# Reordering the first steps of a DeltaNet + hardswish kernel: second norms behind the first group's last score, the inverse's result through SP's queue, query loads between evictions

## The chip, the cores and the metric

The kernel runs on one core of a Trainium2 chip. The metric is device time in microseconds (us). Kernels are compared only within the same rounds.

## The reference

A delta-rule recurrence over 768 tokens, for 4 batches and 8 heads of dimension 48, and then a hardswish MLP over the 3072 resulting tokens (384 to 2048 to 384).

```python
k_n = k / (np.linalg.norm(k, axis=-1, keepdims=True) + 1e-06)
for t in range(S):
    kt, vt, bt = (k_n[:, :, t], v[:, :, t], beta[:, :, t, None])
    y[:, :, t] = np.einsum('bhd,bhde->bhe', q[:, :, t], state)
    v_old = np.einsum('bhde,bhd->bhe', state, kt)
    state = state + bt[:, :, :, None] * np.einsum('bhd,bhe->bhde', kt, vt - v_old)
# ... y, transposed to (tokens, 384), is x
h = x @ w_in
g = h * np.clip(h + 3.0, 0.0, 6.0) / 6.0
out = g @ w_out
```

## The kernel before

The tokens are cut into 24 steps of 32, and the steps into groups of `GS = 4`. Each step has a preparation (`prep`: POOL scales keys, PE transposes keys and queries, ACT copies the transposes out of PE's output memory into `KQ`, which I call evicting, PE makes scores, DVE masks them into `LB`; `kb` are the scaled keys and `mb` the mask times beta, both made by POOL). Each group has its key norms (`norms`) and one triangular inverse on DVE (`inverse`), which collects the group's four `LB` in DRAM, loads them as one matrix `A`, and sends the result back through DRAM (`x_dram`) into the same four `LB`. Then `chain(t)` runs the recurrence; its first matrix product is called `pz`, and `R` is the DVE subtraction that starts every step but the first. The MLP's weights arrive in a format of eight bytes and are converted on the fly by `convert()`: five DVE operations (e, m, m, e and w_in or w_out, after what they write) and one ACT operation (on e) for each of 16 pieces. Steps are counted from 0. `take(x, n)` emits n parts of a generator and `drain(x)` the rest; the order of emission is each engine's order. `need(n)` emits conversions until n are done.

The end of the inverse, and the opening of the program:

```python
def inverse(g, dma):
    ...
    dma.dma_start(out=x_dram[g]..., in_=A...)
    for i in range(GS):
        dma.dma_start(out=LBv[:, :, 0, :], in_=x_dram[g][i]...)
    yield
# ...
for t in range(GS):
    load_k(t)
    load_q(t, nc.scalar)            # all query loads ahead of everything on ACT
for t in range(GS):
    load_k(GS + t)
for i in range(3):
    load_w(i, early)
drain(norms(0, 0, 1))
first = [prep(t, nc.scalar) for t in range(GS)]
take(first[0], 3)
drain(norms(0, 1, GS - 1))
take(first[1])
take(first[0])
inv1 = norms(1, 0, GS)
for t in range(1, GS):
    if t + 1 < GS:
        take(first[t + 1])
    take(first[t], 2)
    if t == 2:
        drain(inv1)                 # second group's norms, ahead of LB(2)
    if t == 3:
        take(conv, 3)
    take(first[t])                  # score and LB(t)
# ...
inv = inverse(0, nc.scalar)         # A, x and its reloads on ACT's queue
take(inv)
need(2)
# ... preps of steps 4 and 5, LB(4)
take(inv, 10)
# ... LB(5)
take(inv, 12)
take(conv)
drain(inv)
take(prep_of(GS + 2), 2)            # transposes and evictions behind the inverse
# ... conversions, preps of steps 6 and 7, chain(0), chain(1)
for n in range(GS):
    load_k(2 * GS + n)              # the third group's keys
need(4)
```

Of the kernel before, what the change touches and what calls it, by code (L numbers as in the profile page):

```python
# [8 lines left out]
FP32 = mybir.dt.float32  # L9
U32 = mybir.dt.uint32  # L10
ACTF = mybir.ActivationFunctionType
# [6 lines left out]
def kernel(  # L18
# [20 lines left out]
    nc = tc.nc  # L39
# [5 lines left out]
    N = S // C  # L45
    NP = H // 2
    GS = 4
# [8 lines left out]
    const = ctx.enter_context(tc.tile_pool(name="const", bufs=1))  # L56
# [8 lines left out]
    def rows(b):  # L65
        return slice(C * b, C * b + C)
# [8 lines left out]
    def tokens(ap, b, t):  # L75
        return ap[b, :, t * C : (t + 1) * C, :].rearrange("h t d -> t h d")
# [10 lines left out]
    def load_q(t, eng=nc.sync):  # L87
        if t < N:
            for b in range(B):
                eng.dma_start(out=qbufs[t % NQB][rows(b), :, 0:D], in_=tokens(q, b, t))  # L90
# [19 lines left out]
    for j, value in enumerate((1.0, -1.0)):  # L110
        m = mask2[:, j, :]
        for b in range(B):
            nc.gpsimd.memset(mask2[rows(b), j, :], value)
            nc.gpsimd.affine_select(
                out=mask2[rows(b), j, :], in_=mask2[rows(b), j, :], pattern=[[1, C]],
                compare_op=ALU.is_gt, fill=0.0, base=0, channel_multiplier=-1,
            )
    half = const.tile([128, 1], FP32, name="half")
    nc.vector.memset(half[:], 0.5)

    beta_tok = persist.tile([P, N, C], FP32, name="beta_tok")
    nc.vector.transpose(out=beta_tok[:].rearrange("p n h -> p (n h)"), in_=beta_hm[:])
# [122 lines left out]
    l_dram, x_dram = {}, {}  # L245
# [57 lines left out]
        KQs[t], LBs[t] = KQ, LB  # L303
        yield

    def inverse(g, dma):

        A = work.tile([128, C, C], FP32, name="A", bufs=1)
        dma.dma_start(
            out=A[:].rearrange("p c i -> p (c i)"),  # L310
            in_=l_dram[g][:].rearrange("t h (b c) i -> (t h b) (c i)", b=B),
        )
        yield
        for j in range(1, C - 1):
            n = C - 1 - j
            pr = work.tile([128, C * C // 4 - C // 2], FP32, name="pr", bufs=1)
            pv = pr[:, 0 : j * n].rearrange("p (c i) -> p c i", c=j)
            nc.vector.tensor_tensor(  # L318
                out=pv, in0=A[:, j, j + 1 :].unsqueeze(1).to_broadcast([128, j, n]),
                in1=A[:, 0:j, j].unsqueeze(2).to_broadcast([128, j, n]), op=ALU.mult,  # L320
            )
            nc.vector.tensor_tensor(  # L322
                out=A[:, 0:j, j + 1 :], in0=A[:, 0:j, j + 1 :], in1=pv, op=ALU.subtract
            )
            yield
        nc.vector.memset(A[:].rearrange("p c i -> p (c i)")[:, 0 : C * C : C + 1], -1.0)
        dma.dma_start(
            out=x_dram[g][:].rearrange("t h (b c) i -> (t h b) (c i)", b=B),
            in_=A[:].rearrange("p c i -> p (c i)"),
        )  # L330
        for i in range(GS):
            LBv = LBs[g * GS + i][:].rearrange("p e a j w -> p (e a) j w")
            dma.dma_start(out=LBv[:, :, 0, :], in_=x_dram[g][i].rearrange("h p c -> p h c"))
        yield


# [115 lines left out]
    def up(blk):  # L452

        xT = xTs[blk]
        for f in range(NFC):
            ph = psM.tile([128, TB], FP32, name="ph", tag="pm")
            for s in range(NKT):
                nc.tensor.matmul(  # L458
                    ph[:], lhsT=w_in[:, s, f * 128 : (f + 1) * 128], rhs=xT[:, s, :],
                    start=(s == 0), stop=(s == NKT - 1),  # L460
                )
            t1 = mlp[0].tile([128, TB], FP32, name="t1", bufs=3)
            nc.scalar.activation(  # L463
                out=t1[:], in_=ph[:], func=ACTF.Relu, bias=half[:, 0:1], scale=1.0 / 6.0
            )
            g = mlp[0].tile([128, TB], FP32, name="g", bufs=NFC + 2)
            nc.vector.scalar_tensor_tensor(  # L467
                out=g[:], in0=t1[:], scalar=1.0, in1=ph[:], op0=ALU.min, op1=ALU.mult
            )
            gs[blk, f] = g  # L470
            yield
# [40 lines left out]
    def need(n):  # L512
        while done[0] < n:
            take(conv)


    def chained(*gens):
        for gen in gens:
            yield from gen

    def take(gen, n=1):
        for _ in range(n):
            next(gen, None)

    def drain(gen):
        for _ in gen:
            pass

    conv = convert()
# [3 lines left out]
    def prep_of(t):  # L533
        if t not in preps:
            preps[t] = prep(t, nc.sync) if t < N else iter(())
        return preps[t]

    with tc.manual_schedule():
        with tc.tile_pool(name="early", bufs=3) as early:
            for t in range(GS):  # L540
                load_k(t)
                load_q(t, nc.scalar)
            for t in range(GS):
                load_k(GS + t)
            for i in range(3):
                load_w(i, early)
            drain(norms(0, 0, 1))
            first = [prep(t, nc.scalar) for t in range(GS)]
            take(first[0], 3)
            drain(norms(0, 1, GS - 1))  # L550
            take(first[1])
            take(first[0])
            inv1 = norms(1, 0, GS)
            for t in range(1, GS):
                if t + 1 < GS:
                    take(first[t + 1])
                take(first[t], 2)
                if t == 2:
                    drain(inv1)
                if t == 3:  # L560
                    take(conv, 3)
                take(first[t])
            load_v(0)
            load_v(1)
            load_w(3)
            inv = inverse(0, nc.scalar)
            take(inv)
            need(2)
            for t in range(2):
                take(prep_of(GS + t), 3)  # L570
            take(prep_of(GS))
            take(inv, 10)
            take(prep_of(GS + 1))
            load_w(4)
            take(inv, 12)
            take(conv)
            drain(inv)
            take(prep_of(GS + 2), 2)
            take(conv)
            take(prep_of(GS + 3), 2)  # L580
            take(conv)
            for t in range(2, GS):
                take(prep_of(GS + t), 2)
                take(conv)
            for t in range(CB):
                load_v(t + 2)
                for _ in chain(t):
                    take(conv)
            for n in range(GS):
                load_k(2 * GS + n)  # L590
            need(4)
        mlp.append(ctx.enter_context(tc.tile_pool(name="mlp", bufs=2)))
        units = mlp_units()
        fill = chained(norms(2, 0, GS), inverse(1, nc.sync))
        for t in range(CB, N):
            g, i = divmod(t, GS)
            load_v(t + 2)
            if i == 1 and (g + 2) * GS < N:
                for n in range(GS):
                    load_k((g + 2) * GS + n)  # L600
            if i == 2 and t > CB:
                drain(fill)
                fill = chained(
                    norms(g + 2, 0, GS) if (g + 2) * GS < N else iter(()),
                    inverse(g + 1, nc.sync) if (g + 1) * GS < N else iter(()),
                )

            now = [prep_of(t + GS + i), prep_of(t + GS + i + 1)] if i < 2 else None
            j = (i + 1) % GS
            later = prep_of(t + 1 + GS + j) if j < 2 else iter(())  # L610
            early = t < GS
            plan = {
                0: lambda: (take(ch), now and take(now[1])),
                2: lambda: now and take(now[1]),
                3: lambda: (take(ch), now and take(now[0])),
                5: lambda: now and take(now[1]),
                7: lambda: (take(ch), now and take(now[1])),
                9: lambda: take(ch),
                11: lambda: take(ch),
                12: lambda: take(later),  # L620
                13: lambda: take(later),
                15: lambda: take(later),
            }
            ch = chain(t)
            for u in range(NU):
                if u in plan:
                    plan[u]()
                if early and u % 2:
                    continue
                if early:  # L630
                    need(min(NWI, ((t - CB) * NU + u) // 4 + 2))
                else:
                    take(conv, 2)
                if early:
                    take(fill, 3)
                take(units)
                if not early:
                    take(fill, 1 + (u % 2 == 0))
            drain(ch)
        drain(units)  # L640
# [30 lines left out]
```

## Time and profile before

| what | us |
|---|---|
| median of the first three runs (779.21 to 779.71) | 779.55 |
| span of the profiled run | 778.0 |
| inverse of the first group: first operation, store of x issued | 48.47, 74.23 |
| first pz of the chain | 84.99 |
| R of step 5, the start of the saturated part | 205.42 |

How to read it: after about 205 us PE is full, so whatever happens earlier is worth only what it moves that moment. The way there is a relay: norms, keys, scores, LB, inverse, chain. A moment of this relay (the start of the inverse, the first pz) is a better ruler than any engine's busy share.

### The profile page before, as it was taken

The numbers are of one execution on the slowest core, as the hardware profiler recorded it, in microseconds if no ns is written. First come the engines' busy times: TensorE is split into PE (matmuls) and PEld (weight loads), VectorE is DVE, ScalarE is ACT, GpSimd is POOL, SyncE is SP. The second block draws the span as 40 slices with busy tenths as digits, with TensorE's granted clock in tenths as the row PEclk, the third lists the DMA queues.
The fourth block names the chain that finished last, engine by engine and source line by source line (L and its number), as shares of the span: only waits on it lengthen the run. The fifth ranks groups of instructions, "written<-read, shape, count | busy, mean of one in ns | idle before, by whom it ended". The sixth has DMA issues, their size and how long they took to land.

```text
span 778.0 us, 24919 instructions
## 1 busy us (share of the span) xinstructions
PE 681.3 (88%) x11208; PEld 501.7 (64%) x11208; DVE 359.1 (46%) x868; ACT 178.0 (23%) x353; POOL 94.8 (12%) x139
## 2 busy tenths in 40 slices
PE   1440686668799999999999999999999999999997
PEld 1330565546576776876876867867868768677674
DVE  6498459968527831247711367511464213021020
ACT  1210321222321231321322311313213113122120
POOL 4750031003004002012011040020000000000000
PEclk9755577789999999999999999999999999999999
DMA  6653740366321131330132501311203010000000
GB/s 122 174 126 89 135 119 7 112 162 187 63 43 52 23 77 35 74 63 18 43 67 44 110 9 27 66 26 30 47 12 81 8 27 6 13 13 0 21 1 20
DMA packets 140139, 45.77 MB, mean 59 GB/s; under 512 B 130272, under 2 KB 133344, under 8 KB 140032
## 3 DMA queue, kind: packets, MB, share of 16 engines
q1 hardware_dynamic: 127008, 41.18, 23.4%
q10 hardware_dynamic: 13024, 2.98, 1.8%
q8 instruction: 88, 1.44, 0.8%
q14 instruction: 19, 0.16, 0.1%
HBM read 33.13 MB, written 11.01 MB: 57 GB/s over the span
## 4 chain that ended last, share of the span: by engine, by line
PE 74%; DVE 14%; DMA 4%; issue 3%; SPq 2%; POOL 2%; ACT 1%; ACTq 0%; POOLq 0%; DVEq 0%
PE po L479 31%; PE ph L458 29%; DVE A L322 3%; DVE pr L318 3%; PE pz L370 2%; PE py L370 2%; PE su L427 2%; PE sc L286 2%; PE ks L360 2%; PE pt L273 2%; DMA kf<-in_k_dram 2%; PE py L360 2%; DVE m L179 1%; DVE e L183 1%; DVE e L168 1%
## 5 line engine op out<-in xcount | busy, mean ns | idle before, releaser
L458 PE MATMUL ph<-xT,w_in 128*128 128x256 f32 x1152 | 277.1, 393 | 15.2 <-DVE w_in L188 9.0
L479 PE MATMUL po<-w_out,g 128*128 128x384 f32 x768 | 265.1, 494 | 4.0 <-DVE w_out L188 4.0
L458 PEld LDWEIGHTS ph<-xT,w_in 128*128 128x128 f32 x1152 | 218.4, 195 | 49.8 <-DVE w_in L188 9.4
L479 PEld LDWEIGHTS po<-w_out,g 128*128 128x128 f32 x768 | 141.3, 191 | 90.3 <-issue 5.2
L467 DVE SCALAR_TENSOR_TENSOR g<-t,ph 128x256 f32<-128x256 f32 x192 | 80.5, 420 | 189.8 <-ACT t L463 189.5
L463 ACT ACTIVATE t<-ph,half 128x256 f32<-128x256 f32 x192 | 90.7, 473 | 189.5 <-PE ph L458 176.2
L322 DVE TENSOR_TENSOR A<-A,pr 128x30 f32<-128x30 f32 (+9 forms) x180 | 68.0, 378 | 6.2
L318 DVE TENSOR_TENSOR pr<-A 128x30 f32<-128x30 f32 (+9 forms) x180 | 66.9, 372 | 4.3
L286 PE MATMUL sc<-KQ 64*32 64x64 f32 x1536 | 22.9, 249 | 43.2 <-ACT KQ L276 42.5
L435 DVE TENSOR_TENSOR state<-state,su 128x384 f32<-128x384 f32 x46 | 23.2, 546 | 71.0 <-PE su L427 71.0
L286 PEld LDWEIGHTS sc<-KQ 64*32 64x32 f32 x1536 | 18.5, 117 | 47.2 <-ACT KQ L276 45.3
L276 ACT ACTIVATE KQ<-pt 128x512 f32<-128x512 f32 x48 | 27.8, 596 | 84.5 <-PE pt L273 64.4
L258 POOL TENSOR_TENSOR mb<-beta_tok,mask 128x256 f32<-128x256 f32 x48 | 32.9, 706 | 82.7 <-DVE LB L292 82.7
L292 DVE TENSOR_TENSOR LB<-sc,mb 128x512 f32<-128x512 f32 x24 | 16.4, 685 | 57.3 <-PE sc L286 57.3
L251 POOL TENSOR_TENSOR kb<-kf,inv 128x384 f32<-128x384 f32 x24 | 21.6, 900 | 163.5 <-PE pt L273 134.1
L209 POOL TENSOR_TENSOR sq<-kf 128x384 f32<-128x384 f32 x21 | 17.4, 827 | 177.8 <-DMA kf<-in_k_dram 101.5
L485 ACT ACTIVATE o<-po 128x384 f32<-128x384 f32 x24 | 11.8, 491 | 111.5 <-PE po L479 111.5
L273 PE MATMUL pt<-ident,kb 128*128 128x128 f32 x96 | 18.3, 320 | 18.7 <-POOL kb L251 17.6
L169 ACT ACTIVATE e<-e,rebias 128x768 uint32<-128x768 uint32 x16 | 15.0, 935 | 80.9 <-DVE e L168 80.9
L386 DVE TENSOR_TENSOR R<-vf,ks 128x384 f32<-128x384 f32 x23 | 12.7, 550 | 37.2 <-PE ks L360 37.2
L273 PEld LDWEIGHTS pt<-ident,kb 128*128 128x128 f32 x96 | 13.5, 164 | 23.2 <-POOL kb L251 18.7
L370 PEld LDWEIGHTS py<-Z,LB 32*32 32x32 f32 x1536 | 19.1, 109 | 14.2 <-issue 12.5
(55 smaller groups left out, 401.9 us busy)
## 6 DMA issues: line engine op xcount, KB each, us to landing
d<-in_moe_w_in_dram SPq DMA_DIRECT2D x8, 768.0 KB, 6.2
d<-in_moe_w_out_dram SPq DMA_DIRECT2D x8, 768.0 KB, 5.7
kf<-in_k_dram SPq DMA_DIRECT2D x96, 48.0 KB, 2.4
vf<-in_v_dram SPq DMA_DIRECT2D x96, 48.0 KB, 2.2
out_dram<-o SPq DMA_DIRECT2D x96, 48.0 KB, 1.6
qb<-in_q_dram SPq DMA_DIRECT2D x80, 48.0 KB, 2.3
l_dram<-LB SPq DMA_DIRECT2D x20, 128.0 KB, 2.4
A<-l_dram SPq DMA_DIRECT2D x5, 512.0 KB
```

The source lines that it names most:

```text
L258: nc.gpsimd.tensor_tensor(out=mb[:, e], in0=beta_tok[:, t, e:H:2].unsqueeze(2).unsqueeze(3).to_broadcast([P, NP, 2, C]), in1=mask2[:].unsq ...
L273: nc.tensor.transpose(pt[:, p, :], src[:, 2 * p : 2 * p + 2].rearrange("p e w -> p (e w)"), ident[:])
L276: nc.scalar.activation(out=KQ[:, :, j, :], in_=pt[:], func=ACTF.Copy)
L286: nc.tensor.matmul(scv[rows(b), e, p], lhsT=KQ[r, p, 0, rows(b)], rhs=KQ[r, p, :, rows(b)], start=True, stop=True,)
L318: nc.vector.tensor_tensor(out=pv, in0=A[:, j, j + 1 :].unsqueeze(1).to_broadcast([128, j, n]), in1=A[:, 0:j, j].unsqueeze(2).to_broadcast( ...
L322: nc.vector.tensor_tensor(out=A[:, 0:j, j + 1 :], in0=A[:, 0:j, j + 1 :], in1=pv, op=ALU.subtract)
L360: nc.tensor.matmul(ph[rows(b), e, D * p : D * p + D], lhsT=KQ[r, p, j, rows(b)], rhs=state[r, b, p, :], start=(p == 0), stop=True, skip_gr ...
L370: nc.tensor.matmul(place(h, b), lhsT=m(h)[rows(b)], rhs=z[rows(b), D * h : D * h + D], start=start, stop=True, skip_group_check=True, tile ...
L458: nc.tensor.matmul(ph[:], lhsT=w_in[:, s, f * 128 : (f + 1) * 128], rhs=xT[:, s, :], start=(s == 0), stop=(s == NKT - 1),)
L463: nc.scalar.activation(out=t1[:], in_=ph[:], func=ACTF.Relu, bias=half[:, 0:1], scale=1.0 / 6.0)
L467: nc.vector.scalar_tensor_tensor(out=g[:], in0=t1[:], scalar=1.0, in1=ph[:], op0=ALU.min, op1=ALU.mult)
L479: nc.tensor.matmul(po[:], lhsT=gs[blk, f][:, c * P : (c + 1) * P], rhs=w_out[:, f, :], start=(f == 0), stop=(f == NFC - 1),)
```

## The change

The intent is to free ACT's queue and to start things in the order in which they are needed: the second norms leave the first group's path, PE's transposes no longer stand behind the inverse's result, and eight query loads leave the head of ACT's queue. The core of the diff (cuts marked; besides, an early ACT operation loads the activation table):

```diff
-    def inverse(g, dma):
+    def inverse(g, dma, back):
...
-        dma.dma_start(            # x_dram <- A
+        back.dma_start(
...
-            dma.dma_start(out=LBv[:, :, 0, :], ...)
+            back.dma_start(out=LBv[:, :, 0, :], ...)
...
                 load_k(t)
-                load_q(t, nc.scalar)
+                if t < 2:
+                    load_q(t, nc.scalar)
...
             take(first[0], 3)
+            load_q(2, nc.scalar)
...
-            inv1 = norms(1, 0, GS)
...
-                if t == 2:
-                    drain(inv1)
+                if t == 1:
+                    load_q(3, nc.scalar)
...
-            inv = inverse(0, nc.scalar)
+            inv = inverse(0, nc.scalar, nc.sync)
             take(inv)
-            need(2)
+            drain(norms(1, 0, GS))
+            need(1)
...
-            take(inv, 12)
+            take(inv, 10)
             take(conv)
+            take(prep_of(GS + 2), 2)
             drain(inv)
-            take(prep_of(GS + 2), 2)
-            take(conv)
+            take(conv, 2)             # and twice more, denser in the same way
...
-                for _ in chain(t):
-                    take(conv)
+                for part, _ in enumerate(chain(t)):
+                    take(conv, 1 + part % 2)
...
-            need(4)
+            need(3)
```

More of the change, by code (lines that the diff above doesn't have):

```diff
@@ L117 @@
             )
-    half = const.tile([128, 1], FP32, name="half")
-    nc.vector.memset(half[:], 0.5)
+    halves = const.tile([128, 2], FP32, name="halves")
+    nc.vector.memset(halves[:], 0.5)
+    half = halves[:, 1:2]
     beta_tok = persist.tile([P, N, C], FP32, name="beta_tok")
@@ L332, in inverse @@
             LBv = LBs[g * GS + i][:].rearrange("p e a j w -> p (e a) j w")
-            dma.dma_start(out=LBv[:, :, 0, :], in_=x_dram[g][i].rearrange("h p c -> p h c"))
+            back.dma_start(out=LBv[:, :, 0, :], in_=x_dram[g][i].rearrange("h p c -> p h c"))
         yield
@@ L463, in up @@
             nc.scalar.activation(
-                out=t1[:], in_=ph[:], func=ACTF.Relu, bias=half[:, 0:1], scale=1.0 / 6.0
+                out=t1[:], in_=ph[:], func=ACTF.Relu, bias=half, scale=1.0 / 6.0
             )
@@ L541 @@
                 load_k(t)
-                load_q(t, nc.scalar)
+                if t < 2:
+                    load_q(t, nc.scalar)
+            nc.scalar.activation(out=half, in_=halves[:, 0:1], func=ACTF.Copy)
             for t in range(GS):
@@ L574 @@
             load_w(4)
-            take(inv, 12)
+            take(inv, 10)
             take(conv)
+            take(prep_of(GS + 2), 2)
             drain(inv)
-            take(prep_of(GS + 2), 2)
-            take(conv)
+            take(conv, 2)
             take(prep_of(GS + 3), 2)
-            take(conv)
+            take(conv, 2)
             for t in range(2, GS):
                 take(prep_of(GS + t), 2)
-                take(conv)
+                take(conv, 2)
             for t in range(CB):
                 load_v(t + 2)
-                for _ in chain(t):
-                    take(conv)
+                for part, _ in enumerate(chain(t)):
+                    take(conv, 1 + part % 2)
             for n in range(GS):
                 load_k(2 * GS + n)
-            need(4)
+            need(3)
         mlp.append(ctx.enter_context(tc.tile_pool(name="mlp", bufs=2)))
         units = mlp_units()
-        fill = chained(norms(2, 0, GS), inverse(1, nc.sync))
+        fill = chained(norms(2, 0, GS), inverse(1, nc.sync, nc.sync))
         for t in range(CB, N):
@@ L604 @@
                     norms(g + 2, 0, GS) if (g + 2) * GS < N else iter(()),
-                    inverse(g + 1, nc.sync) if (g + 1) * GS < N else iter(()),
+                    inverse(g + 1, nc.sync, nc.sync) if (g + 1) * GS < N else iter(()),
                 )
```

## The prediction

> **What bounds the kernel now.** I first read the page's 40 slices, of 19.5 us each, to see which stage has slack. From about slice 11 on TensorE (PE) is full at full clock; before that nothing is. The change touches only the program up to the first two steps of the recurrence, so its worth is how much earlier PE reaches its saturated stretch.
>
> ```profile
> PE   1440686668799999999999999999999999999997
> DVE  6498459968527831247711367511464213021020
> PEclk9755577789999999999999999999999999999999
> ```
>
> Second, busy time by stage. Columns: PE, weight loads, DVE, ACT, POOL, each with a count, then clock, DMA share, GB/s.
>
> ```profile
> 0.00:50.00 50.00, 19.06 (x436) 15.09 (x436) 32.98 (x88) 9.55 (x15) 30.23 (x55) 0.80 0.61 136
> 50.00:75.00 25.00, 1.33 (x8) 0.93 (x8) 23.11 (x62) 0.93 (x1) 3.75 (x5) 0.54 0.48 105
> 75.00:105.00 30.00, 18.55 (x779) 15.19 (x779) 12.60 (x20) 6.88 (x12) 0.83 (x1) 0.50 0.61 125
> 105.00:155.00 50.00, 36.55 (x612) 28.56 (x611) 45.17 (x113) 11.29 (x23) 8.00 (x11) 0.81 0.26 76
> 155.00:205.00 50.00, 37.15 (x616) 26.02 (x619) 38.82 (x58) 15.82 (x27) 8.61 (x8) 0.91 0.57 151
> 205.00:778.00 573.00, 568.68 (x8784) 415.89 (x8770) 206.46 (x533) 133.56 (x275) 43.44 (x60) 1.00 0.18 37
> ```
>
> After 205 us PE is busy 568.68 of 573 us: those 573 us stay. Before it PE idles 205 - 112.6 = 92 us. At 50 to 75 us DVE inverts the first group's matrix; at 75 to 105 us PE and DVE alternate in a serial chain; at 105 to 155 us DVE is the bound (45 of 50 us busy).
>
> Third, the waits of PE up to 210 us, and the order of time on ACT around its longest one:
>
> ```profile
> PE sc L286 <- ACT KQ L276: 42.5, 7, 28.2
> ```
>
> ```profile
> 69.27 0.93 ACT L169 ACTIVATE e<-e,rebias 128x768 uint32<-128x768 uint32 x1 [23.28 <-DVE e L168]
> 74.23 0.34 ACTq L327 DMA_DIRECT2D x_dram<-A  x1
> 76.88 2.41 ACTq L333 DMA_DIRECT2D LB<-x_dram  x4
> 79.33 1.57 ACT L276 ACTIVATE KQ<-pt 128x512 f32<-128x512 f32 x3 [9.13 <-DMA LB<-x_dram]
> ```
>
> PE stands still for 28.2 us because its evictions are behind the store of the inverse in ACT's in-order queue, and that store waits for DVE. After it, two scores, a query transpose and their evictions must run before the first chain product:
>
> ```profile
> 84.99 1.50 PE L370 MATMUL pz<-vf,LB 32*32 32x48 f32 x64
> ```
>
> So 84.99 - 74.23 = 10.8 us pass from the inverse's end to the chain. Fourth, what starts the inverse:
>
> ```profile
> 35.26 0.35 DVE L238 RECIPROCAL inv<-nt 128x32 f32<-128x32 f32 x1
> 35.53 0.63 DVE L292 TENSOR_TENSOR LB<-sc,mb 128x512 f32<-128x512 f32 x1
> 47.87 0.68 DVE L292 TENSOR_TENSOR LB<-sc,mb 128x512 f32<-128x512 f32 x1
> 48.47 0.18 DVE L318 TENSOR_TENSOR pr<-A 128x30 f32<-128x30 f32 x1
> ```
>
> The second group's norms hold up the first group's third LB from 26.6 (its score done) to 35.53. But the LB right ahead of the inverse (47.87) is of step 4, the second group's: it needs those same norms.
>
> **What the Trainium skill says.** "DMA: Bandwidth & Descriptors", section "Issuing engines are not separate DMA queues": DMAs from ACT and SP share the same 16 engines; another issuer only saves sequencer time. The trace agrees that issue time is what there is to free: 2.41 us for four loads, on ACT, plus the waits. "ScalarE: Activation LUTs", section "What ACT_TABLE_LOAD costs": about 1283 ns for the load; the trace has 1.28 us at 12.91. "SBUF — State Buffer", section "Who interferes with whom": a DVE instruction with two SBUF inputs contends with GpSimd reads. The trace agrees: two mb of POOL take 1.19 us beside an idle DVE and 2.22 us beside the conversion at 41.33. "TensorE: Matmul & The Clock Gate", section "What's actually happening": the clock is throttled by default and activity releases it; here 0.50 at 75 to 105 us and 1.00 after 205.
>
> **The change, part by part.** No engine gains or loses work worth naming (one 128x1 copy is added). PE and POOL keep their order exactly; DVE, ACT and SP are reordered.
>
> *Query loads and the table load.* Eight query issues leave the head of ACT's queue: the table load moves from 12.91 to about 8, and the first evictions from 14.20 to about 12.2. Nothing follows: the first LB waits in DVE's order for the norms ending at 18.3. The eight issues return between evictions (four after step 0's, four after step 1's, from 21.95). Here I see a hidden cost. Every DMA waits on a semaphore shared with the DMA eight places earlier in program order, whichever queue issued it. The last key loads and the first raw weight now stand eight places behind these query loads: query issue at about 23.5 to 24, landing 2.4 us later (the page's q row is 2.3), so the first weight load goes out at about 26.2 rather than 21.58. It moves 0.79 MB; from the slice rates around 27 us (some 340 GB/s) it takes 2.3 us plus about 2 us to land: 30.6.
>
> *Norms behind the last score.* LB of step 2 goes from 35.53 to about 26.7, but then come three operations of the first conversion (0.55 + 0.55 + 0.96 = 2.1 us), waiting for that weight: 30.8 to 32.9. Last LB of the group: 33.5 (before 39.78). The matrix A is therefore loaded some 6 us earlier. But the norms now start only at 33.5: four square and reduce pairs at 1.49 us (the spacing of the rows at 27.50 to 31.98) and the 3.0 us tail give 41.5 rather than 35.6. POOL, kb(4), mb, bkb, kb(5): 0.83 + 1.5 + 0.8 + 0.83, to 45.6; transposes 2.0; score 1.2; waits 0.4: LB(4) at 49.3 and the inverse at 50 instead of 48.47. One conversion (4.7 us) is no longer ahead of it, but the norms took its place: +1.5 us. The inverse keeps its 25.7 us (48.47 to 74.2; one LB and one e lie in it in both): end at 75.7.
>
> *X through SP, transposes first.* During the inverse ACT is free, so steps 6 and 7's key transposes, 6's query and its score get done. After the inverse DVE does two m, e, w_in (3.4 us), LB(6), e (1.2 us), ACT its e (0.94); only then does ACT evict the last query transpose (0.6), PE makes the last score (1.2): 7.6 us instead of 10.8: chain at 83.3. The x path (2.65 store, 0.6 issue, 2.2 landing) ends at 81.2, just hidden. Gain so far 1.7 us.
>
> *Denser conversions in the chain.* Step 1's R now waits for a whole w_in: R at 92.6 against 93.09, so 1.2 us of the 1.7 go. The third group's keys, which reuse a raw weight's buffer, must wait for the fifth conversion instead of the fourth: issue from 96.2 against 93.20; that may cost the norms 2 us, but the weight ahead of them has left earlier, so their 16 issues should run faster than 10.41 us. I put the third norms' end 1.5 us ahead of before's 113.7. In return DVE enters its bound stage with one w_in (0.95) and one e, m (1.1) already done: 2 us less in 105 to 155.
>
> Sum at the stage's end: 1.5 + 2.0 = 3.5 us, carried through 155 to 205 (same order, DVE and SP set the pace) and kept by PE: 779.55 - 3.5 = 776.0 us.
>
> **The rivals.** (a) The blocked ACT queue is all of the loss: then the 28.2 us hole closes and the chain starts right after x lands, perhaps earlier too if step 4's LB is early: 8 to 10 us, 770. For it: the longest wait of PE. Against: a hole filled by 5 us of work that PE could do is not 28 us gained; DVE sets the end of the hole. (b) The lane wait and the later norms push the inverse later than I think (third key load too): the inverse starts at 53 or 54, and the result is 779 to 782. For it: the weight's wait is new and DVE's order puts three conversion operations ahead of the last LB. (c) The chain's gain is swallowed at 105 to 155 because the third keys land later, and PE's clock, 0.5 to 0.8 there, does not follow: 778 to 779.5.
>
> **Range and chances.** Centre 776.0 us; 770 from (a) below, 781 from (b) above holds it 8 in 10. A gain of 2% would need 763.9 us, 15.6 us, more than closing the path from inverse to chain entirely; a loss of 2% would need 16 us in the first 100. Faster 0.03, same 0.95, slower 0.02.
>
> **What would show it.** The order of time in the changed kernel: table load near 8 us; first weight issue at 26 rather than 21.6; kb(4) on POOL near 41.7 rather than 35.76; inverse start near 50, end near 75.7; first pz near 83.3; R of step 1 near 92.6; third keys issued from 96; the stage 105 to 155 about 2 us less DVE work; PE full from about 201; and 568 to 573 us after it unchanged. I am wrong if the inverse starts well before 48 (then the norms were not on its path), if the weight goes out at 21.6 (no lane wait), or if the saturated part changes its length.

## The result, and the profile after

The changed kernel took 778.73 us (median of 4 runs, 778.54 to 781.02) against 779.38 us for the kernel before in the same rounds (4 runs, 777.56 to 779.71). The ratio is 1.0003, 95% interval 0.9979 to 1.0028. Ratios here are the mean time of one kernel's runs over that of the other's of the same rounds, so not quite the ratio of the medians that I quote. A second set of runs on another chip (six runs) gave 780.35 us against 779.94, ratio 1.0012 [0.9997, 1.0028]. The change is worth nothing that these runs can measure. The correct output was produced by this and every kernel below.

The slices of the profiled run of the changed kernel (PE, DVE and the granted clock, in tenths, 40 slices):

```profile
PE   1441587558799999999999999999999999999997
DVE  6269859968527731247711367511464213021020
PEclk9995569889999999999999999999999999999999
```

From slice 11 on, PE reads as before, and DVE in all digits but one. Inside the first ten slices the work has moved about, and it comes out at the same place. Busy time by stage of the changed kernel (columns as in the prediction: PE, weight loads, DVE, ACT, POOL, clock, DMA share, GB/s):

```profile
0.00:50.00 50.00, 16.33 (x305) 13.19 (x305) 24.33 (x78) 8.89 (x14) 25.22 (x52) 1.00 0.65 141
50.00:75.00 25.00, 5.96 (x207) 5.07 (x207) 22.06 (x54) 2.99 (x5) 5.88 (x8) 0.60 0.41 93
75.00:105.00 30.00, 16.14 (x714) 13.10 (x712) 20.94 (x39) 5.69 (x10) 0.83 (x1) 0.56 0.65 145
105.00:155.00 50.00, 35.82 (x636) 28.34 (x622) 45.26 (x113) 12.91 (x26) 8.83 (x12) 0.85 0.27 77
155.00:205.00 50.00, 35.62 (x675) 25.34 (x676) 38.04 (x55) 14.73 (x25) 7.77 (x7) 0.90 0.54 141
205.00:777.00 572.00, 567.88 (x8717) 415.07 (x8702) 205.59 (x532) 133.59 (x275) 43.43 (x60) 1.00 0.17 37
```

DVE did 8.65 us less in the first 50 us (32.98 before, 24.33 now) and 8.34 us more between 75 and 105 us. Most of that is conversions taken from ahead of the inverse and put into the chain. In the first 50 us DVE is idle half the time although the way to the inverse runs through it. DVE's order of time in the changed kernel shows why (start, duration, then in brackets the idle time ahead and what ended it):

```profile
27.22 0.69 DVE L293 TENSOR_TENSOR LB<-sc,mb 128x512 f32<-128x512 f32 x1 [3.50 <-POOL sq L210]
...
32.47 0.56 DVE L169 TENSOR_SCALAR e<-d 128x768 uint32<-128x768 uint32 x1 [4.56 <-DMA d<-in_moe_w_in_dram]
...
34.41 0.68 DVE L293 TENSOR_TENSOR LB<-sc,mb 128x512 f32<-128x512 f32 x1
...
42.76 0.35 DVE L239 RECIPROCAL inv<-nt 128x32 f32<-128x32 f32 x1
...
51.29 0.69 DVE L293 TENSOR_TENSOR LB<-sc,mb 128x512 f32<-128x512 f32 x1 [5.87 <-PE sc L287]
51.89 0.18 DVE L319 TENSOR_TENSOR pr<-A 128x30 f32<-128x30 f32 x1
```

LB(2) is 8.3 us earlier than before (27.22 against 35.53), but DVE then stands for 4.56 us until the first raw weight is there, because three operations of a conversion come ahead of LB(3). Only then come the norms, whose last operation is at 42.76 (35.26 before). The keys, transposes and score of step 4 follow, and DVE stands 5.87 us for that score. LB(4) is at 51.29, and the inverse, right behind it, starts at 51.89: 3.4 us later than before.

The weight is late because its load is. On SP's queue, before and after (one line of each kernel's order of time):

```profile
21.58 1.52 SPq L156 DMA_DIRECT2D d<-in_moe_w_in_dram  x3
```

```profile
26.84 1.52 SPq L157 DMA_DIRECT2D d<-in_moe_w_in_dram  x3
```

The key loads ahead of it in SP's queue now wait for query loads that ACT issues. In the waits of SP's queue from 10 to 40 us, this line of the changed kernel (total us, times, longest) has no counterpart before:

```profile
SPq L85 <- DMA qb<-in_q_dram: 6.7, 3, 3.3
```

The program as built tells the reason: its eight completion semaphores serve all DMAs in turn, and a DMA waits for the one eight places earlier in program order, on whichever queue ("the lane wait" below). At the other end of the inverse, the changed kernel's SP queue, and then its ACT and PE orders of time:

```profile
77.64 0.34 SPq L328 DMA_DIRECT2D x_dram<-A  x1
...
80.28 2.38 SPq L334 DMA_DIRECT2D LB<-x_dram  x4
```

```profile
81.98 0.94 ACT L170 ACTIVATE e<-e,rebias 128x768 uint32<-128x768 uint32 x1 [8.52 <-DVE e L169]
82.82 0.58 ACT L277 ACTIVATE KQ<-pt 128x512 f32<-128x512 f32 x1
```

```profile
83.45 1.19 PE L287 MATMUL sc<-KQ 64*32 64x64 f32 x64 [7.71 <-ACT KQ L277]
84.57 1.50 PE L371 MATMUL pz<-vf,LB 32*32 32x48 f32 x64
```

From the store of x to the first pz are 6.9 us (84.57 - 77.64), 10.8 before. So the second half of the change earned 3.8 us (10.76 - 6.93), the first half lost 3.4 us, and the chain starts 0.4 us earlier.

### The profile page after: what moved, and what is told of

Same layout as the page of the kernel before. It is cut to its first block, busy times and chain, and to the rows that moved or that the text cites. A ratio compares the mean times of both kernels' runs of the same rounds, so it can differ in the third digit from the quotient of the medians.

```text
span 777.2 us, 24923 instructions
## 1 busy us (share of the span) xinstructions
PE 677.8 (87%) x11208; PEld 500.1 (64%) x11208; DVE 356.2 (46%) x868; ACT 178.8 (23%) x354; POOL 92.0 (12%) x139
## 4 chain that ended last, share of the span: by engine, by line
PE 76%; DVE 12%; issue 3%; DMA 3%; POOL 3%; SPq 1%; ACT 1%; POOLq 0%; DVEq 0%; ACTq 0%
PE po L480 32%; PE ph L459 30%; DVE A L323 3%; DVE pr L319 3%; PE pz L371 2%; PE py L371 2%; PE su L428 2%; PE sc L287 2%; PE pt L274 2%; PE ks L361 2%; PE py L361 2%; DMA kf<-in_k_dram 1%; DMA d<-in_moe_w_in_dram 1%; DVE e L184 1%; DVE m L180 1%
## 5 line engine op out<-in xcount | busy, mean ns | idle before, releaser
L459 PE MATMUL ph<-xT,w_in 128*128 128x256 f32 x1152 | 273.8, 390 | 18.1 <-DVE w_in L189 10.2
L464 ACT ACTIVATE t<-ph,halves 128x256 f32<-128x256 f32 x192 | 90.9, 474 | 194.1 <-PE ph L459 183.0
```

Of the source, the lines that this page charges most:

```text
L459: nc.tensor.matmul(ph[:], lhsT=w_in[:, s, f * 128 : (f + 1) * 128], rhs=xT[:, s, :], start=(s == 0), stop=(s == NKT - 1),)
L464: nc.scalar.activation(out=t1[:], in_=ph[:], func=ACTF.Relu, bias=half, scale=1.0 / 6.0)
```

## The experiments

Theory: the change is the sum of a good half (x through SP with the transposes ahead of it, the conversions put off) and a bad half (norms and query loads moved), and the bad half costs by two links: the weight's load behind the query loads, and LB(4), which needs the second norms, standing in DVE's order right ahead of the inverse. First rival: the good half earns nothing by itself, because the x path or the clock swallows it. Second rival: the moved norms are right, and only the query loads hurt. The first four runs are one batch on one chip.

### x through SP alone

The kernel before with only this:

```diff
-            inv = inverse(0, nc.scalar)
+            inv = inverse(0, nc.scalar, nc.sync)
...
-            drain(inv)
             take(prep_of(GS + 2), 2)
+            drain(inv)
             take(conv)
```

> The kernel before with only the inverse's store and reload moved to SP and step 6's transposes put ahead of it. Theory (the x part is the useful part; norms and query loads only delay the inverse): inverse starts at 48.5 us and ends at 74.2 as before, both score steps are done during it, first pz near 80 instead of 85.0, time 774.5 to 776.5 us. Rival A (any gain ahead of 155 us is swallowed downstream by the w_out loads): pz near 80 but the time within 1 us of before. Rival B (the ACT queue was not what held PE): pz still near 85.

Measured: 775.59 us (773.15 to 777.29, six runs) against 778.41, ratio 0.9964 [0.9939, 0.9989]. The inverse is where it was (x stored at 73.95). Its SP queue, and its PE:

```profile
73.95 0.34 SPq L327 DMA_DIRECT2D x_dram<-A  x1
76.69 2.45 SPq L333 DMA_DIRECT2D LB<-x_dram  x4
```

```profile
79.06 1.50 PE L370 MATMUL pz<-vf,LB 32*32 32x48 f32 x64 [3.51 <-issue]
```

Now 5.1 us pass from the store to pz, and pz waits for no eviction. So the first rival is wrong. The two parts of this edit, the queue and the order of step 6's transposes, were not run apart; what the order alone would give is not shown. The gain at pz is 5.9 us, of which about half reaches the end (0.36% of 778.41 is 2.8 us). Some of it is lost on the way: the third keys are issued only 1.9 us earlier than before (91.28 against 93.20), behind value loads and a weight in SP's queue, and R of step 5 is 4.4 us earlier (201.05). The two profiled runs are 4.6 us apart (773.4 and 778.0 us of span), so the step from 4.4 to 2.8 is a difference between runs and not a loss that a trace shows.

### Query loads back at the head

The changed kernel with all four query loads at the head of ACT's queue again.

```diff
-                if t < 2:
-                    load_q(t, nc.scalar)
+                load_q(t, nc.scalar)
...
-            load_q(2, nc.scalar)
...
-                if t == 1:
-                    load_q(3, nc.scalar)
```

> The changed kernel with all four query loads again at the head of ACT's queue. Theory (the query loads between evictions delay the first raw weight through the shared DMA semaphores): first weight issue back at 21.6 us instead of 26.8, first conversion no longer waits for it, last LB of the first group near 31.0 instead of 34.4, inverse start near 48.5 instead of 51.9, time 775 to 776.5 us. Rival: the weight's issue stays near 26.8 or the inverse start stays near 51.9, time as the changed kernel, 778 to 779.

Measured: 775.39 us (774.15 to 777.37), ratio 0.9963 [0.9942, 0.9984]. The weight goes out at 21.68, and the wait of SP's key loads for query loads shrinks to 0.5 us in all. On DVE, LB(3) and LB(4):

```profile
30.27 0.69 DVE L293 TENSOR_TENSOR LB<-sc,mb 128x512 f32<-128x512 f32 x1 [0.82 <-PE sc L287]
...
47.14 0.69 DVE L293 TENSOR_TENSOR LB<-sc,mb 128x512 f32<-128x512 f32 x1 [5.86 <-PE sc L287]
```

Both are 4.1 us earlier than in the changed kernel, and so is the first pz (80.42). The weight's wait is thereby shown to be on the path, and to be worth 4.1 us there. The profiled run was the slowest of its six, so I take from it the early moments only.

### The norms back ahead of LB(2)

The changed kernel with the second norms where they were.

```diff
+            inv1 = norms(1, 0, GS)
...
+                if t == 2:
+                    drain(inv1)
...
             take(inv)
-            drain(norms(1, 0, GS))
             need(1)
```

> The changed kernel with only the second norms put back ahead of step 2's LB. Theory (step 4's LB, which needs these norms, gates the inverse): kb of step 4 near 35.8 us instead of 43.3, inverse start near 46.3 (then A's load is the limit) instead of 51.9, first pz near 79, time 773 to 775.5 us. Rival (the norms were rightly moved: A's early load matters): inverse start not earlier than 50, time 778 or more. Rival A (swallowed downstream): start near 46 but time within 1 us of before.

Measured: 773.19 us (770.55 to 774.31), ratio 0.9926 [0.9904, 0.9948]. The weight still goes out late (26.14) and costs nothing: DVE is at the norms meanwhile, and LB(3) is at 38.63, where the next kernel with its early weight has it at 38.68. The inverse starts at 45.95, now behind the load of A itself:

```profile
45.95 0.19 DVE L319 TENSOR_TENSOR pr<-A 128x30 f32<-128x30 f32 x1 [1.20 <-DMA A<-l_dram]
```

That is 5.9 us ahead of the changed kernel, the first pz is 6.7 us ahead (77.88 against 84.57), and R of step 5 is 6.0 us ahead. The second rival is wrong: the moved norms hurt more than the query loads do.

### Both back

Both edits above together: of the change, x through SP with the transposes, the early table load and the conversions' new places remain.

> Both undone: what is left of the change is x through SP, the transposes ahead of it and the denser conversions (one conversion instead of two ahead of the inverse). Theory: as the kernel with early norms, since the weight's delay then lies beside the norms: inverse start near 46.3, pz near 79, time 773 to 775.5, and 1 to 2 us faster than x alone because one conversion less lies ahead of the inverse. Rival: denser conversions give the gain back in the chain of the first two steps, so no faster than x alone.

Measured: 772.65 us (771.19 to 773.88), ratio 0.9926 [0.9906, 0.9947]; the inverse starts at 45.86, the first pz is at 78.25. With the norms early the place of the query loads makes no difference. With them late it makes some 0.4%. Read as a table of ratios against the kernel before (the lower right cell from two other batches):

| | query loads at the head | query loads spread |
|---|---|---|
| norms ahead of LB(2) | 0.9926 | 0.9926 |
| norms behind the last score | 0.9963 | 1.0003 and 1.0012 |

So x through SP is worth -0.36%; the conversions' new places, with what else remains, bring that to -0.74% (the inverse starts 2.4 us earlier than with x alone, 45.86 against 48.21, with one conversion fewer ahead of it); the moved norms take 0.37 points back, and the query loads the rest. Each interval is about 0.2% wide to either side. That these steps add up to the whole is no test, as they are differences along one way through the table; along the other way the query loads cost nothing and the norms all of it.

### Can the norms' move be made to pay?

The move loses because DVE does step 4's LB before the inverse. If that is so, ten steps of the inverse ahead of LB(4) should win it back. This run and the next three are one batch (779.40 us for the kernel before). First the changed kernel with that edit alone:

```diff
-            take(prep_of(GS))
             take(inv, 10)
+            take(prep_of(GS))
+            take(inv, 4)
             take(prep_of(GS + 1))
             load_w(4)
-            take(inv, 10)
+            take(inv, 6)
```

> The changed kernel with one edit: ten steps of the inverse ahead of step 4's LB instead of behind it. Theory (A is there at about 42 us and only the order on DVE keeps the inverse waiting): inverse start near 45.5 us instead of 51.9, LB of step 4 still near 51.3, inverse end near 71.5 instead of 77.6, first pz near 79, time 773 to 775.5 us. Rival (A or POOL's work, not the LB's place, gates it): start at 50 or later, time as the changed kernel, 778 to 779.

Measured: 777.66 us (776.2 to 778.65), ratio 0.9975 [0.9962, 0.9989]. The start is 6.8 us earlier than in the changed kernel, at 45.14, as the theory has it. The time is not the 773 to 775.5 us that I had put down; it lies just under the 778 to 779 us of the rival, whose mechanism the start refutes. x is stored at 74.62, only 3.0 us earlier. LB(4) now comes in the inverse's middle, and later than the 51.3 us expected,

```profile
55.12 0.68 DVE L293 TENSOR_TENSOR LB<-sc,mb 128x512 f32<-128x512 f32 x1
```

and the inverse takes 29.5 us from first operation to store instead of 25.7. Most of that is not LB(4): the sixty operations of the inverse's own steps take 26.05 us in all instead of 22.80, and they now begin while POOL prepares steps 4 and 5 (the next experiment shows such operations). Here the theory of the start holds, and my size for the end does not.

### An early A

From the kernel with both moved back: the norms split (sums of squares ahead of LB(3), the rest behind it), the first conversion behind them, and the same ten steps of the inverse first.

```diff
-                if t == 2:
-                    drain(inv1)
                 if t == 3:
-                    take(conv, 3)
+                    take(inv1, 4)
                 take(first[t])
+            drain(inv1)
...
-            take(prep_of(GS))
             take(inv, 10)
+            take(prep_of(GS))
+            take(inv, 4)
             take(prep_of(GS + 1))
             load_w(4)
-            take(inv, 10)
+            take(inv, 6)
```

> The version with front query loads, now with the second norms split (reductions ahead of the first group's last LB, tail after it), the first conversion after the norms, and ten steps of the inverse ahead of step 4's LB. Theory (the inverse's start is the lever; it was gated by step 4's LB and then by A's load): A's load near 36 us, inverse start near 41 instead of 45.9, end near 67 instead of 71, first pz near 74, time 768.5 to 770.5 us. Rival (the rest of the start, key loads and the SP queue, sets the pace once the inverse is early): inverse early but time 772 or more.

Measured: 772.74 us (771.87 to 774.72), ratio 0.9921 [0.9906, 0.9936], which is not told apart from the 0.9926 of its parent. The inverse starts at 41.44, 4.4 us earlier than in the parent, and x is stored at 69.83, only 1.5 us earlier: a miss of the end, and the time is that of the rival (772 or more). The inverse now begins while POOL prepares steps 4 and 5, and its sixty operations take 24.96 us instead of the parent's 22.51. One line of POOL, and one of DVE, in this run:

```profile
36.99 2.21 POOL L259 TENSOR_TENSOR mb<-beta_tok,mask 128x256 f32<-128x256 f32 x2
```

```profile
41.44 0.81 DVE L319 TENSOR_TENSOR pr<-A 128x30 f32<-128x30 f32 x1
```

The same first operation of the inverse takes 0.18 us in the kernel before, where POOL stands until 48.64, and the two mb take 1.19 us beside an idle DVE. Operations of both engines are longer here where they overlap, as the prediction had read of conversions; an early start bought in this way is partly paid in duration.

The 1.5 us that are left at the first pz (76.75 against 78.25) go in the second chain step, and not for a reason that the theory or the rival names: PE pauses for 2.38 us in the middle of a product, waiting for nothing that the trace shows, where the parent's PE does not, and R of step 2 is at 98.13 against 96.69. The kernel before has this pause too (2.79 us), and so has the first profile of the changed kernel (2.43), but not its second. So it may be chance of this one profile; why all six runs together gain nothing stays open.

### All transposes and scores in the inverse

From the kernel with both moved back:

```diff
             take(prep_of(GS + 2), 2)
-            drain(inv)
-            take(conv, 2)
             take(prep_of(GS + 3), 2)
-            take(conv, 2)
-            for t in range(2, GS):
-                take(prep_of(GS + t), 2)
-                take(conv, 2)
+            take(prep_of(GS + 2))
+            take(prep_of(GS + 3))
+            drain(inv)
+            take(prep_of(GS + 2))
+            take(prep_of(GS + 3))
+            take(conv, 8)
```

> The version with both undone, with all four transposes of steps 6 and 7 evicted during the inverse and both LB right behind it, ahead of the conversions. Theory (between inverse and chain the last eviction waited behind a conversion's activation on ACT): first pz at x's store plus 5.1 us, near 76.5 instead of 78.25, time 771 to 772.3 us. Rival: pz near 76.5 but no gain in time, as the conversions behind it then hold the first state update.

Measured: 772.13 us (769.2 to 773.01), ratio 0.9900 [0.9882, 0.9917]. From the store of x (71.84) to pz (77.03) are now 5.2 us rather than the parent's 6.9: what remained between inverse and chain in the changed kernel was the conversion's e operation on ACT ahead of the last eviction, and it can be removed. Whether the end gains by it is less sure: the parent's 0.9926 [0.9906, 0.9947] is from another batch, and the intervals overlap.

### The same with an early A and early keys

The two kernels just told joined, and the third keys loaded ahead of the chain instead of behind it:

```diff
+            for n in range(GS):
+                load_k(2 * GS + n)
             for t in range(CB):
                 load_v(t + 2)
...
-            for n in range(GS):
-                load_k(2 * GS + n)
```

> Early A, scores in the inverse, and the third group's keys loaded ahead of the first two steps of the recurrence (into the second group's key buffer). Theory: inverse start near 41, first pz near 72, the third norms no longer wait for keys, time 766 to 769 us. Rival (w_out loads and DVE in 105 to 205 us swallow it): 769 to 771.

Measured: 770.4 us (768.62 to 773.41), ratio 0.9886 [0.9867, 0.9905]. Both are misses, as pz had been put near 72 and the time at 766 to 769 us; the time is in the rival's 769 to 771, but the first loss found lies ahead of the stretch that the rival names. pz is at 74.85. A new wait has come: SP's queue carries the sixteen key loads ahead of the sixth weight, and DVE stands for that weight in the second chain step. SP's queue and DVE's order of time in this run:

```profile
76.67 11.24 SPq L85 DMA_DIRECT2D kf<-in_k_dram  x16
...
91.45 0.40 SPq L157 DMA_DIRECT2D d<-in_moe_w_in_dram  x1
```

```profile
97.31 0.56 DVE L169 TENSOR_SCALAR e<-d 128x768 uint32<-128x768 uint32 x1 [4.70 <-DMA d<-in_moe_w_in_dram]
```

R of step 2, behind it, is at 98.25 in this run and at 95.97 in the one before, although its chain had started 2.2 us earlier.

### Fewer conversions in the second step

```diff
-                    take(conv, 1 + part % 2)
+                    take(conv, 1 + (1 - t) * (part % 2))
```

> The version with early keys, with one conversion operation instead of one or two at each part of the second step of the recurrence, so that the sixth weight's first two operations no longer stand ahead of R of step 2 (they waited 4.70 us for their load there). Theory: R of step 2 near 94 us instead of 98.25, the second inverse starts near 103.5 instead of 107.2, time 766.5 to 769 us. Rival (the two operations come back later as DVE work in the bound stage, and the load is late anyway): second inverse earlier but time within 1 us of the version before.

Measured: 768.79 us (767.85 to 770.92, five runs) against 779.94 on this chip, ratio 0.9868 [0.9848, 0.9887]. The DVE wait for the sixth weight is gone, R of step 2 is at 93.84 and R of step 5 at 193.81 (205.42 before). It has the lowest ratio and is faster than both kernels. That the last edit by itself gains time is shown by the moments of the trace only: the interval overlaps that of the version before it (0.9867 to 0.9905).

### The changed kernel again

The changed kernel, unedited, ran beside that one. ("R of step 6" in the text put down is R of step 5.)

> The changed kernel itself, timed again in five rounds beside the kernel before, as the first comparison's interval (0.9979 to 1.0028) is wider than the difference in question. Theory (the trace shows 0.8 us less at R of step 6): ratio between 0.997 and 1.0005. Rival (the change is worth its 0.5%): 0.995 or less.

Measured: as told with the result, 1.0012. This profiled run shows how much chance there is inside: x of the second inverse is stored at 155.01, 1.6 us later than in the first profile of the same program (153.45), and R of step 5 is at 204.51 against 204.62. What is won or lost at 155 us by that much need not arrive at 205 us.

The first pz and the end, run by run (us earlier than in the kernel before, 84.99, by each profile; and the ratio's deviation from 1 times the median before of the same rounds):

| kernel | inverse starts | pz earlier by | time less by |
|---|---|---|---|
| changed | 51.89 | 0.4 | -0.2 |
| x through SP alone | 48.21 | 5.9 | 2.8 |
| query loads at the head | 47.75 | 4.6 | 2.9 |
| norms early | 45.95 | 7.1 | 5.8 |
| both back | 45.86 | 6.7 | 5.8 |
| changed, inverse first | 45.14 | 3.4 | 1.9 |
| early A | 41.44 | 8.2 | 6.2 |
| scores in the inverse | 46.36 | 8.0 | 7.8 |
| all, early keys | 41.36 | 10.1 | 8.9 |
| all, second step sparser | 41.26 | 10.2 | 10.3 |

The first pz nearly orders the kernels, and between about a half and all of a gain there reaches the end. The clearest exception is the early A, 8.2 us earlier at pz and 6.2 at the end, where the row below it has 8.0 and 7.8. The start of the inverse alone does not order them (the changed kernel with the inverse first started it earlier than the two kernels in the rows above and gained a third as much).

## Why the prediction was right or wrong

The predicted time was 776.0 us and the measured one 778.73: inside the range and in the class held most likely, but the central gain of 3.5 us did not appear (0.65 us between the medians, 0.8 us between the profiled spans, nothing by the ratio). To lie inside the range says little, as it holds the kernel before's own time too. Three terms of the sum were mis-sized: the weight's landing, the third norms' end, and what is carried from 155 to 205 us. Point by point:

- **Table load and first evictions.** Right: 7.92 us and 11.90 us (about 8 and 12.2 predicted), and nothing follows from it.
- **The lane wait.** Right in mechanism: the first weight goes out at 26.84 us (26.2). The term behind it was mis-sized: "2.3 us plus about 2 us to land: 30.6". It landed 5.6 us after its issue, at 32.4 (DVE, which waits for it, starts at 32.47), with three loads of 768 KB in flight and other loads around it; the working had counted the bytes of one. That is 1.8 us on the path; the query experiment shows that the 4.1 us by which LB(3) was late carry to the first pz whole.
- **Norms to inverse.** Right in mechanism, and the train behind the late start has the sizes worked out: LB(3) ends at 35.09 us (33.5), keys of step 4 at 43.26 (41.7), LB(4) 8.0 us behind them (7.6 had been allowed). The start is at 51.89 us, not 50: the 1.6 us of LB(3) carried, and 0.4 more from there to LB(4). So the loss at the start was 3.4 us and not 1.5. The inverse's length of 25.7 us is right.
- **From inverse to chain.** About right: 6.9 us from the store of x (77.64) to pz (7.6 predicted), with ACT's e operation ahead of the last eviction as described. This error is of the other sign and hides 0.7 us of the one before: pz at 84.57 us rather than 83.3. The gain of "1.7 us" so far was 0.4.
- **Denser conversions in the chain.** R of step 1 at 93.66 us (92.6) and the keys at 97.04 (96.2) follow with about the same error. "Third norms' end 1.5 us ahead" failed: the second inverse, behind them, starts 0.35 us later than before (114.26 against 113.91), and in the second profile of the changed kernel at 115.83. Their sixteen key loads did not make up for the late start, as had been hoped: the last issues end at 106.6 us against 103.6, and POOL, which squares the keys, waits for a key load until 106.38. The 2 us less of DVE work did come: the second x is stored 1.6 us earlier (153.45 against 155.05), so that stage gave 1.95 us, and in the second profile 1.96.
- **Carried through 155 to 205.** This step failed: "carried ... and kept by PE" became half, 0.8 us of 1.6. DVE's wait for the w_out load grew by 1.5 us. DVE before, and after:

```profile
170.74 0.56 DVE L168 TENSOR_SCALAR e<-d 128x768 uint32<-128x768 uint32 x1 [3.04 <-DMA d<-in_moe_w_out_dram]
```

```profile
169.01 0.56 DVE L169 TENSOR_SCALAR e<-d 128x768 uint32<-128x768 uint32 x1 [4.55 <-DMA d<-in_moe_w_out_dram]
```

  But R of step 4, ahead of that wait, had been 3.2 us early (156.19 against 159.43), so 1.7 us are left behind it. The rest goes on PE, whose next chain product waits for an eviction that stands behind the same conversion's e on ACT. PE before, and after:

```profile
172.80 0.88 PE L370 MATMUL pz<-R,LB 32*32 32x48 f32 x64 [2.63 <-ACT KQ L276]
```

```profile
171.07 1.50 PE L371 MATMUL pz<-R,LB 32*32 32x48 f32 x64 [4.17 <-ACT KQ L277]
```

  Behind the longer wait pz takes 1.50 us instead of 0.88, and the score after it 1.18 instead of 0.86; that is the 0.9 us by which the lead shrinks to 0.8 at the next LB (173.80 against 174.58). The granted clock, the share of full speed that PE was allowed, is 0.50 from 171.0 to 173.7 us, and was 1.00 before from 172.8 to 175.0. The twelve profiles agree: where this wait is 2.60 to 2.92 us (five profiles) pz takes 0.88 us, and where it is 3.62 to 5.04 (seven) 1.37 to 1.50. The second run of the changed kernel, with shorter waits (3.02 us for the load, 2.92 for the eviction), came to the same 204.5 us from a later x. No experiment took one of these links away.
- **The saturated part.** Right in length: 572 us from 205 us on with PE busy 567.88 (573 and 568.68 before). It begins with R of step 5 at 204.62 us and not at about 201.

Of the rivals, (b), the later inverse, came nearest, at 51.89 us instead of 53 or 54. Of (c), whose 778 to 779.5 us hold the measured time, the later keys are seen, and they took the chain's lead; what (c) did not have is that DVE's shorter stage behind them gave 1.95 us, of which half was lost later. Rival (a) does not describe this change, but there is truth in it: the blocked queue, undone together with the order of the transposes, is worth 5.9 us at the chain and 2.8 us at the end. The prediction had both signs, 1.5 us lost at the inverse's start and 3.2 won behind it; the record shows 3.4 lost and 3.8 won. What I did not see is that 0.7% were to be had by leaving out the half that the change is named for first.

## What to carry to other kernels

When work is moved off one group's path, look at what stands next in the same engine's order and needs it: here the norms left LB(2) and landed ahead of LB(4), which stood directly ahead of the inverse. When a bundle of edits moves the time by nothing, undo its parts one at a time: a gain and a loss of equal size look like no effect. Loads put between other work can hold up loads on another queue, so compare the issue time of the first large load before and after.

## What the Trainium skill lacked or had wrong

- "DMA: Bandwidth & Descriptors", section "Issuing engines are not separate DMA queues", says that another issuing engine saves only the sequencer time of the issue. Here the issue is 2.4 us for four loads, but the edit that moves x to another queue, and the transposes ahead of the wait, brought the first pz forward by 5.9 us (the two were not run apart): what was freed is the stretch in which ACT's queue stood at a store waiting for DVE and evictions stood behind it, a PE hole of 28.2 us before. The section leaves out the wait of the issued DMA.
- "DMA: Bandwidth & Descriptors", section "🔬 Why a DMA increments its semaphore by 16 and not by 1", treats two DMAs on one semaphore as a question of correctness, and I found no page with its cost in time. In this program eight semaphores are shared by all DMAs, and spreading eight query loads of ACT held up key loads on SP for 6.7 us and moved the first weight's issue from 21.58 to 26.84 us.
